# Re-ordering the second half of a fused RWKV6 + MLP kernel: a projection product in the front of a step, a multiplication inside the near products, and one chunk of unit 4 multiplied a step later

## The chip, the cores and the metric

The kernel runs on one core of one Trainium2 chip. The metric is the device time of one launch in microseconds. Three runs of the kernel before gave 609.04, 611.66 and 611.67 us, a median of 611.66 us. The execution that the profiler recorded took 610.0 us, with a span of 607.9 us from its first to its last instruction.

## The reference

Two blocks follow each other. The first is a linear attention with a decaying state, for 4 batches, 8 heads, 768 tokens and head size 48:

```python
for t in range(S):
    kt, vt, rt, wt = (k[:, :, t], v[:, :, t], r[:, :, t], w[:, :, t])
    cur = np.einsum('bhd,bhe->bhde', u[None] * kt, vt)
    y[:, :, t] = np.einsum('bhd,bhde->bhe', rt, state + cur)
    state = wt[:, :, :, None] * state + np.einsum('bhd,bhe->bhde', kt, vt)
```

Its output, seen as 3072 tokens by 384 features, is the input `x` of the second block, whose inner size is 2048:

```python
h = x @ w_in
sp = np.maximum(h, 0.0) + np.log1p(np.exp(-np.abs(h)))   # softplus
g = h * erf(sp)
return g @ w_out
```

Everything is float32.

## The kernel before, in words

**Units and steps.** The 3072 tokens are cut into 12 units of 256 tokens (two batches of 128 tokens each). One step of the main loop (line 1037) handles one unit of attention, and beside it the MLP of earlier units: in step s the attention of unit s runs, the hidden layer of unit s-1 (`hidden`, line 737) and the output projection of unit s-3 (`project_fast`, line 863, for units from 4 on; `project`, line 787, for the units before). Steps 0 to 4 use one schedule (`attend`), steps 5 to 11 another (`attend_late`, line 570). A tail after the loop finishes the last units. Only steps 5 to 11 are touched by the change.

**The order is written by hand.** The scheduler is off (line 1016), so each engine executes its instructions in the order in which the program issues them. `run_late` (line 967) reads strings of tokens from the tables `LATE` (line 950) and `USUAL` (line 962), one string for each of the places in a step at which `attend_late` calls `run`. The tokens are:

- P: one piece of the projection. In `project_fast` a unit has 7 pieces, each 8 products of 192 columns (line 878), which the trace shows as 16 matmul records. The pieces use two PSUM tiles `m`. Piece 1 is followed by a ScalarE copy (line 884), piece 3 by line 889, piece 4 by line 892, piece 6 by a VectorE addition (line 898) and piece 7 by another (line 902); the last two are followed by a store to HBM on SP's queue. In `project` a unit has 8 pieces, and pieces 6 and 8 are followed by a ScalarE copy (line 811).
- H: one piece of the hidden layer, 12 matmul records (line 770), then a ScalarE copy of 512 columns from PSUM tile `m` to `h` (line 779). A unit has 8. There are only two PSUM tiles `m`, so each H waits for the copy of the H before the last one, and the first two for the last readers of the projection's tiles.
- s, e, m: softplus (line 726), erf (line 730) and multiplication (line 735, VectorE) of one chunk of 1024 columns of `h`. A unit has 4 chunks; a chunk is complete after the 2nd, 4th, 6th and 8th H. Softplus and erf each come with a load of ScalarE's function table. The erf goes to a free PSUM room, called a lane: `ey` uses the tile `y`, `ep` uses the tile `pp1`. The next use of a lane waits for the multiplication that reads it. The first two chunks of a unit are worked on in the step of their H, the others in the step after.
- k: a ScalarE copy of a quarter of the activated unit to a lane (line 838). S: sums and differences of quarters on VectorE (lines 855 to 861), which `project_fast` needs because it forms the 2x2 block product with seven instead of eight products.
- F: the next part of the generator `prepare(s+1)` (line 267). T, G: one of four sums of quarters of `w_out`, on VectorE or GpSimd (line 826). A: one stage of the activation of a unit before 4.

**A step of `attend_late`, on TensorE.** It begins with what is called the front here: `from_own` with swap 1 for the unit before (line 484, 32 matmul records, into `y`), the level 5 products (line 450, 64 records), `from_own` with swap 0 (32 records), which may begin only when a small VectorE copy called the fence has read `y` (line 493), and `through_state` (line 510, 64 records). `from_own` with swap 1 overwrites `y`, so it waits for the last reader of that lane. The level 5 products wait for VectorE's scaling of level 4 (line 263), which is in the last part of `prepare`. Then come most of the P, the level 6 products (line 450) with `spread_blocks` (line 549), the last two P, the state products (line 536) and eight H.

**A step on VectorE.** After the fence it scales level 5 (line 263), takes the level (line 462), and then has a long row from `prepare(s+1)`, the near products: line 384, eight multiplications of distances 1 to 4 (lines 377 and 381), reductions of distances 1 to 3 (line 367), line 396 and two more reductions. GpSimd forms the products of distances 5 to 15 (the same two lines) and begins when the reductions of 1 to 3 have freed a room. Then come line 592 (`kT`), multiplications m, the scaling of level 6, the additions of the projection, the scalings of levels 1 to 3, S, further reductions and the scaling of level 4.

**A step on ScalarE.** It copies `y` to `xT` after `through_state` (lines 517 to 520), runs softplus and erf, copies `few` (line 555) and level 6 (line 469), copies quarters (line 838), and empties the tiles `m`.

**SP's queue** carries nearly all transfers. After `through_state` it issues six small transfers into `xT` (line 524) and then the loads of the next step (`load_step`).

Of the kernel before, what the change touches and what calls it, by code (L numbers as in the profile page):

```python
# [17 lines left out]
P = 128  # L18
# [21 lines left out]
DIRECT = 4  # L40
# [6 lines left out]
def view(ap, offset, dims):  # L47

    return bass.AP(ap.tensor, ap.offset + offset, [ap.ap[0], *dims])
# [12 lines left out]
def kernel(  # L62
# [107 lines left out]
    def near_log(s):  # L170
        return NEAR_LOG - (s == DIRECT)
# [76 lines left out]
    def rows(e, n=D):  # L248
        return slice(e * EP, e * EP + n)
# [17 lines left out]
    def prepare(s):  # L267
# [77 lines left out]
        front = att.tile([P, 2, JP, C], FP32, name="rk1", bufs=1)  # L345
        back = wide.tile([P, 2, DM, 2], I32, name="words", bufs=3)
        front = front[:].rearrange("p x n t -> p (x n t)")
        back = back[:].rearrange("p x n two -> p (x n two)").bitcast(FP32)
        terms, near = {}, 1 << near_log(s)
# [15 lines left out]
        def sum_up(*distances):  # L365
            for n in distances:
                nc.vector.tensor_reduce(  # L367
                    out=view(
                        sums[:], n, [[near * (NEAR + 1), NEAR // near], [NEAR + 1, near - n]]
                    ),  # L370
                    in_=terms[n], axis=mybir.AxisListType.X, op=ALU.add,
                )

        def term(engine, *distances):

            for n in distances:
                engine.tensor_mul(terms[n], r[:, :, n:], k[:, :, : near - n])  # L377

                m = near - n - (s == DIRECT)
                if m:  # L380
                    engine.tensor_mul(k[:, :, :m], k[:, :, :m], w[:, :, n : n + m])  # L381
# [3 lines left out]
        if near < NEAR:  # L385
            term(nc.vector, 1, 2, 3)
            yield
            term(nc.vector, 4, 5, 6, 7)
            nc.vector.tensor_mul(terms[0], terms[0], r)
            yield  # L390
            sum_up(*range(near))
        else:
            term(nc.vector, 1, 2, 3, 4)
            sum_up(1, 2, 3)
            term(nc.gpsimd, 5, 6, 7, 8)
            nc.vector.tensor_mul(terms[0], terms[0], r)
            sum_up(0, 4)
            term(nc.gpsimd, *range(9, NEAR))
# [145 lines left out]
    def spread_blocks(s, pp):  # L544
# [23 lines left out]
        )  # L568

    def attend_late(s, run):  # L570

        c, in_t, vt, own, S, S_next, ends = parts_of(s)
        RK = in_t[:, 0:2]
        before = s - 1 if s - 1 > DIRECT else None
        if before:
            from_own(before, ready[before][0], 1)
            fence()
        pp = products([P, NE, JP, HC], 0)
        level_products(pp, RK, LOG - 1)
        scale(s, LOG - 1)  # L580
        take_level(own, pp, LOG - 1)
        if before:
            from_own(before, ready[before][0], 0)
            through_state(before, xTs[before])
            if s + 1 < n_steps:
                load_step(s + 1)
        following = prepare(s + 1) if s + 1 < n_steps else iter(())
        next(following, None)
        nc.gpsimd.tensor_mul(faded[0][:], S[:], ends[:, :, 0:1].to_broadcast([P, JP, D]))
        next(following, None)  # L590
        kT = kTs[s]
        nc.vector.tensor_mul(
            kT[:].rearrange("p (e n) d -> p n e d", e=NE),
            kT[:].rearrange("p (e n) d -> p n e d", e=NE), spread[s][:],
        )
        run(0, following)

        pp = products([P, NE, JP, HC], 0)
        level_products(pp, RK, LOG)
        if s + 1 < n_steps:  # L600
            spread_blocks(s + 1, pp)
        take_level(own, pp, LOG)
        scale(s, LOG)
        run(1, following)
        ps = products([P, NC, JP, HC], 0)
        ps = [ps[:, h] for h in range(NC)]
        state_part(s, kT, ps)
        run(2, following)
        for e in range(NE):
            nc.vector.tensor_add(middle[rows(e)], faded[0][rows(e)], ps[0][rows(e), :, :D])  # L610
        run(3, following)
        if s < n_steps - SPC:
            nc.gpsimd.tensor_mul(
                faded[1][:], middle[:], ends[:, :, 1:2].to_broadcast([P, JP, D])
            )
            for e in range(NE):
                nc.vector.tensor_add(S_next[rows(e)], faded[1][rows(e)], ps[1][rows(e), :, :D])
        run(4, following)
# [318 lines left out]
    def in_order(s, k):  # L937
# [3 lines left out]
        for what in order[k]:  # L941
# [5 lines left out]
                piece(hids, s - 1)  # L947


    LATE = {  # L950
        DIRECT + 1: (
            "A P P P A P P", "F F F A P P P", "T", "H H F", "A s H ey m H H F G s H ep H H"
        ),
        DIRECT + 2: (
            "m s P P ey m P s P P ep m P", "k22y P F P k11p F F", "S1", "S2 S3 H k12y S4 H F",
            "s H ey m H H F G G s H ep H H",
        ),
        n_steps - 1: (
            "m s P ey m P s P P ep m P", "P P", "S", "H H", "s H ey m H H s H ep H H"
        ),  # L960
    }
    USUAL = (
        "m s P ey m P s P P ep m P", "k22y P F P k11p F F", "S1", "S2 S3 H k12y S4 H F",
        "s H ey m H H F s H ep H H",
    )

# [49 lines left out]
    with tc.manual_schedule(  # L1016
        engines={getattr(mybir.EngineType, x) for x in ("PE", "DVE", "Activation", "Pool", "SP")}
    ):
        warm = ps_m.tile([P, P], FP32, name="m")
        for _ in range(20):  # L1020
            nc.tensor.matmul(warm[:], lhsT=ident[:], rhs=ident[:], start=True, stop=True)  # L1021
        for t in (*states[0], *states[1], middle):
            nc.gpsimd.memset(t[:], 0.0)
        nc.gpsimd.memset(over_blocks[:], 1.0)
        nc.scalar.copy(u_row[:, :1], ident[:, :1])
        for _ in prepare(0):
            pass
        conversion = convert(
            [
                (into[:, f : f + 2, :], given[:, f : f + 2, :])  # L1030
                for into, given in ((w_in_sb, w_in), (w_out_sb, w_out))
                for f in range(0, NT, 2)
            ]
        )
        next(conversion)
        load_step(1)
        for s in range(n_steps):
            xTs[s] = xs.tile([P, KT, UNIT], FP32, name="xT")
            places = iter(range(8))

            def convert_at(n):
                if s < len(CONVERT) and n < len(CONVERT[s]):
                    for what in CONVERT[s][n]:
                        conversion.send(what)

            def place(n):
                if n == LOG - 1 and DIRECT - 1 <= s <= DIRECT:
                    load_rows(s + 2)
                for due in {(3, 4): (5,), (4, 3): (6,), (4, 5): (7,)}.get((s, n), ()):
                    load_w(due)  # L1050
                if s >= DIRECT:
                    in_order(s, next(places))
                    return
                if s in ALONE:
                    if s == 2 and not n:

                        next(hids[0])
                    convert_at(n)
                    advance(STAGES[s][n])
                elif s:  # L1060
                    advance(STAGES[s][n])
                    convert_at(n)
                else:
                    convert_at(n)
                beside(s, next(places))

            def run(n, following):
                if n == 3 and s < n_steps - 2:
                    load_rows(s + 2)
                if n == 3 and s + 3 < n_steps:  # L1070
                    load_w(s + 3)
                run_late(s, LATE.get(s, USUAL)[n], following)

            if s > DIRECT:
                attend_late(s, run)
                continue
            def behind(n=0):
                if n is not None:
                    convert_at(LOG + 2)
                    return  # L1080
                for what in BEHIND_SCALING:
                    conversion.send(what)

            attend(s, xTs[s], place, behind)
            if s + 2 < n_steps:
                load_step(s + 2)
                if s + 2 == DIRECT:
                    load_rows(s + 2)
        s = n_steps
        from_own(s - 1, ready[s - 1][0], 1)  # L1090
        fence()
        run_late(s, "s P")
        from_own(s - 1, ready[s - 1][0], 0)
        through_state(s - 1, xTs[s - 1])
        run_late(s, "m ey m P s P P ep m P P P S H H s H ey m H H s H ep m H H")
        run_late(s + 1, "s P ey m P s P P ep m P P P S")
        run_late(s + 2, "P P P P P P P")
# [96 lines left out]
```

## Time and profile before

| | |
|---|---|
| median of three runs | 611.66 us |
| the profiled execution, its own time | 610.0 us |
| its span | 607.9 us |
| TensorE matmul busy | 589.4 us, 97% of the span |
| VectorE, ScalarE, GpSimd busy | 442.9, 352.3, 281.4 us |
| start of the fronts of steps 6 to 11 | 249.97, 298.74, 345.25, 391.06, 436.85, 482.64 us |
| start of the tail | 526.57 us |

The profile names each instruction by its source line. "Busy" is the time in which an engine executes, and the idle time ahead of an instruction is put down to what released it. A releaser "issue" means that the engine waited for nothing that the profile shows. In the timelines the columns are the start in microseconds, the duration of the merged row, the engine, the line, the operation, what it writes and reads, the count, and in brackets the idle time ahead of the row with its releaser. The queue "q8 instruction" is not issued by the program[...].

### The profile page before, as it was taken

Reading aid. Unit: us, or ns where it says so; the run is one execution under the profiler, and the core shown is the slowest. Engines: PE = TensorE matmul, PEld = TensorE weight load, DVE = VectorE, ACT = ScalarE, POOL = GpSimd, SP = SyncE. Lnnn points to the kernel's source line nnn. Section 1 sums busy time; section 2 is a strip of 40 time slices with the busy share of each in tenths; the row PEclk is TensorE's granted clock in tenths of the full one; section 3 lists DMA queues with packets and bytes.
Section 4 is the critical chain, followed back from the end, with each engine's and each line's share of the span. In section 5 each row is a group of like instructions: output and inputs, shape, how many; then the busy total and the mean of one; then the engine's idle time right before and its main releaser. Section 6 shows DMA issues by size and latency. Waiting matters only on the chain.

```text
span 607.9 us, 16532 instructions
## 1 busy us (share of the span) xinstructions
PE 589.4 (97%) x7242; PEld 496.9 (82%) x7242; DVE 442.9 (73%) x508; ACT 352.3 (58%) x461; POOL 281.4 (46%) x298
## 2 busy tenths in 40 slices
PE   8889999999999999899999999999999999999997
PEld 7668787678668768658898799799898898898997
DVE  5688597895995898999899799799799634114140
ACT  2647887635536536456656666666756774655810
POOL 4348275602497489669749349349349100000000
PEclk9999999999999999899999999999999999999999
DMA  8376471441333413325324324333321300000000
GB/s 323 120 280 215 154 256 59 200 142 18 138 92 121 128 49 143 49 101 182 56 103 167 71 104 167 70 104 133 72 102 54 72 8 27 1 21 14 2 26 27
DMA packets 51376, 63.33 MB, mean 104 GB/s; under 512 B 34920, under 2 KB 40296, under 8 KB 49896
## 3 DMA queue, kind: packets, MB, share of 16 engines
q1 hardware_dynamic: 50824, 62.03, 31.6%
q8 instruction: 57, 0.93, 0.6%
q10 hardware_dynamic: 480, 0.25, 0.2%
q14 instruction: 15, 0.12, 0.1%
HBM read 52.39 MB, written 8.69 MB: 100 GB/s over the span
## 4 chain that ended last, share of the span: by engine, by line
PE 77%; DVE 14%; issue 5%; ACT 3%; POOL 1%; DMA 0%; DVEq 0%; ACTq 0%; POOLq 0%
PE m L770 35%; PE m L878 18%; PE m L802 11%; PE pp L450 6%; DVE in L263 3%; DVE words L381 2%; DVE sums L367 2%; PE y L484 2%; PE m L1021 1%; DVE rk L377 1%; PE y L510 1%; PE pp L536 1%; DVE own L462 1%; PE pp L675 1%; DVE h L735 1%
## 5 line engine op out<-in xcount | busy, mean ns | idle before, releaser
L770 PE MATMUL m<-xT,w_in_sb 128*128 128x256 f32 x1152 | 258.4, 382 | 4.6 <-DVE o L898 1.9
L770 PEld LDWEIGHTS m<-xT,w_in_sb 128*128 128x128 f32 x1152 | 215.6, 190 | 38.5 <-issue 3.5
L779 ACT COPY h<-m 128x512 f32<-128x512 f32 x96 | 55.6, 581 | 84.2 <-PE m L770 83.8
L263 DVE TENSOR_TENSOR in<-in,tot_sb 128x1024 f32<-128x1024 f32 (+1 forms) x60 | 84.7, 1411 | 18.7 <-PE pp L450 17.5
L381 POOL TENSOR_TENSOR words<-words,rest 128x528 f32<-128x528 f32 (+10 forms) x77 | 84.7, 1100 | 6.0
L802 PE MATMUL m<-w_out_sb,h 128*128 128x384 f32 x256 | 85.5, 490 | 0.0
L377 POOL TENSOR_TENSOR rk<-words 128x528 f32<-128x528 f32 (+3 forms) x28 | 35.4, 1264 | 92.3 <-DVE sums L367 81.9
L802 PEld LDWEIGHTS m<-w_out_sb,h 128*128 128x128 f32 x256 | 47.7, 190 | 31.7
L730 ACT ACT_TABLE_LOAD x32 | 41.1, 1283 | 25.7 <-DVE h L735 24.4
L450 PEld LDWEIGHTS pp<-in 48*64 48x64 f32 (+1 forms) x2368 | 34.8, 128 | 15.2 <-issue 8.3
L878 PE MATMUL m<-w_out_sb,h 128*128 128x192 f32 x256 | 44.9, 329 | 0.2 <-issue 0.2
L878 PE MATMUL m<-mixed,h 128*128 128x192 f32 x256 | 44.8, 328 | 0.0
L450 PE MATMUL pp<-in 48*64 48x64 f32 (+1 forms) x2368 | 39.5, 215 | 3.8 <-DVE in L263 1.5
L878 PEld LDWEIGHTS m<-w_out_sb,h 128*128 128x128 f32 x256 | 41.7, 190 | 1.0 <-issue 0.4
L735 DVE TENSOR_TENSOR h<-h,pp 128x1024 f32<-128x1024 f32 x16 | 19.5, 1216 | 31.1 <-ACT pp L730 31.1
L878 PEld LDWEIGHTS m<-mixed,h 128*128 128x128 f32 x256 | 41.7, 190 | 0.3
L726 ACT ACT_TABLE_LOAD x32 | 41.1, 1283 | 0.6
L315 POOL TENSOR_TENSOR tot_sb<-tot_sb 128x256 f32<-128x256 f32 (+4 forms) x60 | 38.1, 636 | 4.5
L377 POOL TENSOR_TENSOR words<-words 128x336 f32<-128x336 f32 (+6 forms) x49 | 38.2, 780 | 3.8
L735 DVE TENSOR_TENSOR h<-h,y 128x1024 f32<-128x1024 f32 x16 | 19.5, 1217 | 28.0 <-ACT y L730 27.8
L878 PE MATMUL m<-w_out_sb,room 128*128 128x192 f32 x224 | 38.7, 326 | 0.0
L878 PEld LDWEIGHTS m<-w_out_sb,room 128*128 128x128 f32 x224 | 36.8, 190 | 0.0
(123 smaller groups left out, 835.2 us busy)
## 6 DMA issues: line engine op xcount, KB each, us to landing
in<-in_rkw SPq DMA_DIRECT2D x11, 1024.0 KB, 5.1
words<-in_moe_w_in SPq DMA_DIRECT2D x8, 768.0 KB, 5.8
words<-in_moe_w_out SPq DMA_DIRECT2D x8, 768.0 KB, 4.6
words<-in_rk_rows SPq DMA_DIRECT2D x8, 768.0 KB, 5.6
w<-in_rkw SPq DMA_DIRECT2D x11, 512.0 KB, 7.0
v<-in_v SPq DMA_DIRECT2D x12, 384.0 KB, 6.2
out<-o SPq DMA_DIRECT2D x24, 192.0 KB, 2.6
rest<-in_w_rows SPq DMA_DIRECT2D x8, 384.0 KB, 6.0
```

The source lines that it names most:

```text
L263: nc.vector.tensor_mul(halves, halves, view(tots[level - 1], 0, [[1, n], [2, nb], [0, half]]))
L315: nc.gpsimd.tensor_mul(new, pair[:, :, 0], pair[:, :, 1])
L377: engine.tensor_mul(terms[n], r[:, :, n:], k[:, :, : near - n])
L381: engine.tensor_mul(k[:, :, :m], k[:, :, :m], w[:, :, n : n + m])
L450: nc.tensor.matmul(pp[s0 : s0 + m, e, n, :m], lhsT=rk[rows(e), 1, n, s0 : s0 + m], rhs=rk[rows(e), 0, n, t0 : t0 + m], start=True, stop=True,)
L726: nc.scalar.activation(sp_room, chunks[0], AF.Softplus)
L730: nc.scalar.activation(at, sp_room, AF.Erf)
L735: nc.vector.tensor_mul(h, h, at)
L770: nc.tensor.matmul(ps[:, ff, :], lhsT=w_in_sb[:, g * FG + f + ff, kk * P : (kk + 1) * P], rhs=xT[:, kk, :], start=kk == 0, stop=kk == KT - 1,)
L779: nc.scalar.copy(h[:, f : f + FT, :], ps[:])
L802: nc.tensor.matmul(ps[j][:], lhsT=gs[g][:, f, j * C : (j + 1) * C], rhs=w_out_sb[:, g * FG + f, :], start=g + f == 0, stop=g == NG - 1 and ...
L878: nc.tensor.matmul(to, lhsT=a[:, f], rhs=b[:, f], start=start and f == 0, stop=f == FG - 1, skip_group_check=True,)
```

## The change

The order of the work is changed in steps 5 to 11; no instruction of any engine is added or removed by its text.

- `prepare` gets one more stop, between the multiplications of distances 1 to 4 and the reductions, for steps from 6 on.
- `attend_late` calls `run` at two more places: "front", between the level 5 products and `from_own` with swap 0, and "near", at the new stop in `prepare`.
- In steps 6 to 11 the front now holds a softplus and one P. The multiplication of the second chunk of the unit, which was the first token after line 592, is now in "near". The last multiplication stands behind the level 6 scaling instead of ahead of it.
- In step 5 only one chunk of unit 4 is activated instead of two: its erf goes to lane `pp1` instead of `y`, and it is multiplied in step 6. The other three chunks of this unit each move one place on, so that the softplus and the erf of the last one stand among the last two P of step 6, and the lanes of step 6 are exchanged.

```diff
@@ -391,6 +391,8 @@
             sum_up(*range(near))
         else:
             term(nc.vector, 1, 2, 3, 4)
+            if s > DIRECT + 1:
+                yield
             sum_up(1, 2, 3)
             term(nc.gpsimd, 5, 6, 7, 8)
             nc.vector.tensor_mul(terms[0], terms[0], r)
@@ -579,6 +581,7 @@
         level_products(pp, RK, LOG - 1)
         scale(s, LOG - 1)
         take_level(own, pp, LOG - 1)
+        run("front", None)
         if before:
             from_own(before, ready[before][0], 0)
             through_state(before, xTs[before])
@@ -587,6 +590,8 @@
         following = prepare(s + 1) if s + 1 < n_steps else iter(())
         next(following, None)
         nc.gpsimd.tensor_mul(faded[0][:], S[:], ends[:, :, 0:1].to_broadcast([P, JP, D]))
+        next(following, None)
+        run("near", None)
         next(following, None)
         kT = kTs[s]
         nc.vector.tensor_mul(
@@ -947,20 +952,21 @@
+    STAGES_LATE = ("front", "near", 0, 1, 2, 3, 4)
     LATE = {
         DIRECT + 1: (
-            "A P P P A P P", "F F F A P P P", "T", "H H F", "A s H ey m H H F G s H ep H H"
+            "", "", "A P P P A P P", "F F F A P P P", "T", "H H F", "A s H H H F G ep H H H"
         ),
         DIRECT + 2: (
-            "m s P P ey m P s P P ep m P", "k22y P F P k11p F F", "S1", "S2 S3 H k12y S4 H F",
-            "s H ey m H H F G G s H ep H H",
+            "s P", "m", "ey P m s P P ep P m P", "s P P F ey m k22p k11y F F", "S1",
+            "S2 S3 H k12p S4 H F", "s H ey m H H F G G s H ep H H",
         ),
         n_steps - 1: (
-            "m s P ey m P s P P ep m P", "P P", "S", "H H", "s H ey m H H s H ep H H"
+            "s P", "m", "ey P m s P P ep P", "m P P", "S", "H H", "s H ey m H H s H ep H H"
         ),
     }
     USUAL = (
-        "m s P ey m P s P P ep m P", "k22y P F P k11p F F", "S1", "S2 S3 H k12y S4 H F",
+        "s P", "m", "ey P m s P P ep P", "m k22y P F P k11p F F", "S1", "S2 S3 H k12y S4 H F",
         "s H ey m H H F s H ep H H",
     )
@@ -1069,7 +1075,7 @@
-                run_late(s, LATE.get(s, USUAL)[n], following)
+                run_late(s, LATE.get(s, USUAL)[STAGES_LATE.index(n)], following)
```

`DIRECT` is 4, so the three entries of `LATE` are those of steps 5, 6 and 11, and `USUAL` is that of steps 7 to 10. The tail's strings are unchanged.

## The prediction

> **What bounds the kernel now.** I read the busy shares first, then TensorE's timeline of steps 9 and 10, then VectorE's and ScalarE's for the one wait that stands there, and last the boundary of steps 5 and 6. The page says that TensorE sets the time: it is busy in 97% of the span, at full clock nearly everywhere, so a gain can only come from its gaps.
>
> ```profile
> PE 589.4 (97%) x7242; PEld 496.9 (82%) x7242; DVE 442.9 (73%) x508; ACT 352.3 (58%) x461; POOL 281.4 (46%) x298
> PEclk9999999999999999899999999999999999999999
> q8 instruction: 57, 0.93, 0.6%
> ```
>
> TensorE's timeline from 384 to 478 us shows the step of about 45.8 us and three kinds of gap.
>
> ```profile
> 392.93 0.52 PE L510 MATMUL y<-in,s 48*48 48x64 f32 x24
> 394.67 0.32 PE L510 MATMUL y<-in,s 48*48 48x64 f32 x7 [1.23 <-issue]
> ...
> 459.28 0.92 PE L536 MATMUL pp<-v,kT 64*48 64x48 f32 x32
> 461.13 13.35 PE L770 MATMUL m<-xT,w_in_sb 128*128 128x256 f32 x60 [0.94 <-DVE o L898]
> 474.68 3.50 PE L770 MATMUL m<-xT,w_in_sb 128*128 128x256 f32 x15 [0.20 <-ACT h L779]
> ```
>
> (1) The front stops in the middle of equal small matmuls with the releaser "issue". Numbering TensorE's records in the trace (weight loads, matmuls, semaphores), the stops of steps 6 to 9 come after number 7617, 8641, 9665 and 10689, exactly 1024 apart. A q8 packet starts 2.3 to 2.4 us before each restart: 252.18, 301.00, 346.68, 392.30 us against restarts at 254.62, 303.33, 349.12, 394.67. There are 57 packets of 16 KB for 14,593 records, 256 each. So the next 256 instructions had not arrived. In the four stops the 256 records up to the restart took 3.1 to 3.6 us; the front's 192 weight-load and matmul pairs run at 15 ns each, 256 records in under 2 us, which is faster. Lost: 0.3, 0.3, 1.4 and 1.4 us.
>
> (2) The first H waits for VectorE's line 898. VectorE's and ScalarE's rows in step 10 say why it is late:
>
> ```profile
> 452.75 1.73 DVE L592 TENSOR_TENSOR kT<-kT,spread 128x768 f32<-128x768 f32 x1
> 454.40 1.21 DVE L735 TENSOR_TENSOR h<-h,pp 128x1024 f32<-128x1024 f32 x1
> 455.53 1.21 DVE L735 TENSOR_TENSOR h<-h,y 128x1024 f32<-128x1024 f32 x1
> 458.04 1.22 DVE L735 TENSOR_TENSOR h<-h,pp 128x1024 f32<-128x1024 f32 x1 [1.30 <-ACT pp L730]
> 459.17 1.44 DVE L263 TENSOR_TENSOR in<-in,tot_sb 128x512 f32<-128x512 f32 x1
> 460.54 0.54 DVE L898 TENSOR_TENSOR o<-o,m 128x384 f32<-128x384 f32 x1
> ```
>
> ```profile
> 455.68 1.28 ACT L730 ACT_TABLE_LOAD   x1 [4.93 <-DVE h L735]
> 456.98 1.03 ACT L730 ACTIVATE pp<-room 128x1024 f32<-128x1024 f32 x1
> ```
>
> The erf of the last chunk needs lane `pp1`, which the second chunk's multiplication frees only after all near products. ScalarE idles 4.93 us, then VectorE 1.30 us, and line 898 follows two instructions later. TensorE loses 1.1 us in steps 7 and 10. In steps 8 and 9 gap (1) has made TensorE late enough to hide this: the two gaps are rivals for the same time.
>
> (3) Into step 6, TensorE stands from 247.88 to 249.97 us, and again at 251.1:
>
> ```profile
> 249.97 0.90 PE L484 MATMUL y<-own,v 64*48 64x64 f32 x32 [1.94 <-DVE h L735]
> 251.13 1.99 PE L450 MATMUL pp<-in 48*64 48x64 f32 x64 [0.25 <-DVE in L263]
> ```
>
> ```profile
> 243.39 5.27 DVE L759 TENSOR_TENSOR h<-h,room 128x1024 f32<-128x1024 f32 x2
> 248.70 1.22 DVE L735 TENSOR_TENSOR h<-h,y 128x1024 f32<-128x1024 f32 x1
> 249.84 1.23 DVE L263 TENSOR_TENSOR in<-in,tot_sb 128x1024 f32<-128x1024 f32 x1
> ```
>
> `from_own` overwrites lane `y`, whose reader stands behind two slow multiplications; the level 4 scaling stands behind that reader. The windows show the price: a clock of 0.63 from 250 to 251 us and 0.50 from 251 to 253.
>
> [...] the trace has half clock for 3.41 us from 250.25 on, after only 2.1 us of idling. [...] line 759 took 3.29 us beside GpSimd's 3.44 us line 826, against its mean of 1.81.
>
> **The change part by part.** Nothing is added to any engine, so I lay the same rows out in the new order. T is the start of a front.
>
> *P in the front.* TensorE in a usual step: 0.48 + 0.93 (the first `from_own`, level 5), P 2.7, then 0.45 + 1.00, four P 10.6, level 6 and line 549 0.94, two P 5.4, state 0.87, H 20.92: together 44.3 us. A stretch of 256 instructions can no longer miss a P (2.7 us for 32 instructions): 2.7 + 224 x 7.5 ns = 4.4 us at least, above the 3.1 to 3.6 us that a block needs. All stops in fronts go: 0.3 + 1.4 + 1.4 = 3.1 us in steps 7 to 9. Splitting the row of P costs something: a P next to small tiles takes 2.80 us in the tail (row of line 878 at 527.16) against 2.64 in a row of five, so 0.2 us a step. What moves with it: the softplus stands in ScalarE's queue ahead of the `y` copies, but ScalarE idles there 2.3 to 3.8 us, and the copies wait for line 510 anyway. They come 2.7 us later, and so do SP's six transfers and `load_step` behind them: these end near T + 11, and H asks for `xT` at T + 23; the loads land about 5 us after issue and are asked for at T + 23 as well. No cost. GpSimd's queue isn't passed by these.
>
> *m inside the near products.* On VectorE line 592 begins at T + 15.9 now (452.75 - 436.85), then at T + 17.0. Behind it: 1.65 (kT), 1.13 (m), 1.38 (level 6 scaling), 1.13 (last m), 0.54 (line 898) = T + 22.9, against T + 24.2 now. The first H asks for its tile at T + 23.4. So gap (2) closes with 0.5 us to spare. The last erf: lane `pp1` is free at T + 12.2, line 892 waits for the fourth P until T + 13.9, table load and erf take 2.33, done at T + 16.3, and VectorE asks at T + 21.2. The copies k22 and k11 wait for the last m as before (T + 22.3; now 22.4). GpSimd's far products start 1.14 us later, and with them the reductions of their last terms; those lead to the level 4 scaling, which then has 2.3 us in hand. With VectorE 1.3 us earlier, the wait of 0.36 us inside H (steps 7 and 10) goes too.
>
> Steps 7 to 10 took 482.64 - 298.74 = 183.9 us. Now 4 x (44.3 + 0.2 + 0.1 for what small waits stay) = 178.4. **Minus 5.5 us.** Summed by gaps: 3.1 + 2.6 + 0.7 - 0.8 = 5.6.
>
> *Unit 4's first chunk a step later.* Step 5 no longer uses `y`, so `from_own` starts at 247.88. Level 5 still waits for line 263, which now follows line 759 directly: 248.70 to 249.93. TensorE idles 1.6 us there (from 248.36 to 249.98). This idling is between those of 1.4 us, after which the clock held, and the 2.1 us that halved it; I take full clock and keep 1.5 us for the other case. The front without P then takes 2.10 + 0.93 + 1.45 = 4.5 us, instead of 7.11 (247.88 to 254.99). With the split 0.2: **minus 2.4 us.**
>
> *The price in step 6.* The last chunk's erf now stands behind the copy of the eighth P (line 811) in ScalarE's queue. The P end at 274.4. Then line 811 to 275.0, table load and erf to 277.4, m to 278.6, k22 and k11 to 280.5, and only then the first H's line 779, to 281.1; the third H wants its tile at 280.5. The next copy, k12, waits for S1 (VectorE: scalings 3.1 to 3.5, S1 1.2, so 283), and the second H's copy stands behind it. Followed on, waits of 0.65, 0.7 to 1.0, 0.3 and 0.3: **plus 2.1 us**; bounds 0 (if ScalarE catches up) and 3.
>
> Step 11: no stop now, one split: plus 0.2. The tail: nothing. Sum: -5.5 - 2.4 + 2.1 + 0.2 = -5.6 us. On the profiled execution 610.0 - 5.6 = 604.4 us. The median of the runs is 1.66 above that execution and the mean of all four is 610.6; I say **605.0** for a median.
>
> **Rivals.**
> *More is gained (602.7):* step 6's queue costs nothing, -2.1. For it: in the old step 6 H ran without a gap. Against: the chain above has five links without slack.
> *Half is gained (608.0):* the spare 0.5 us before line 898 is used up, so a wait of about 0.9 us comes back at the first H in four steps (3.6 us less gain), or the half clock stays (1.5) and part of the fetch stops reappears elsewhere, the change then not doing what its front is shaped for. For it: in step 7 line 263 took 1.93 us instead of 1.23. Against: steps 8 to 10 agree to 0.1 us.
> *Slower (617):* GpSimd's far products, 1.14 us later, block two of VectorE's two-input instructions (lines 396, 592, 263) for 1.5 us each, as line 759 was blocked. Then line 898 is 3.0 us later in each of five steps, and 5 x (3.0 - 0.5) = 12.5 against 5.6 gained. It decides from 0.5 us a step, and the sign turns at 1.6. Against: these lines run beside the same GpSimd rows now, line 592 at 1.6 to 1.7 us.
>
> **How the numbers follow.** 605.0 (603.5 to 607): 0.55; 602.7: 0.18; 608.0: 0.20; slower: 0.07. The range 602.0 to 609.0 leaves out the slower case and the edges. About 0.5%, 3 us, can be told from no change; half of the third case falls inside. So faster 0.80, same 0.13, slower 0.07.
>
> **What would show it.** Right: no "issue" gap in the fronts of lines 484 to 510, steps 7 to 10 at 44.6 us, line 898 ended before line 536 ends, 1.6 us ahead of level 5 in step 6, waits for line 779 in step 6's H. Wrong: an "issue" gap at another line, a first H that waits for line 898, or half clock after step 5.

## The result, and the profile after

| | before | changed |
|---|---|---|
| median of six runs | 610.14 us (609.04 to 611.67) | 605.58 us (603.82 to 607.62) |
| profiled execution, its own time | 610.0 us | 603.8 us |
| its span | 607.9 us | 602.0 us |
| mean TensorE clock in it (1.0 is full clock) | 0.997 | 1.0 |

The ratio is 0.9922, with a 95% interval of 0.9894 to 0.995: 0.8% faster. In the changed kernel the lines from 394 on have moved by 2, those from 582 on by 3, those from 590 on by 5 and those of the tables and behind them by 6: the level 5 and 6 products are now line 452, `from_own` 486, `through_state` 512, softplus 731, erf 735, the multiplication m 740, the two multiplications of a token A 764, the H matmuls 775 and their copy 784, the products of `project` 807 and its copy 816, the copy of a quarter 843, the first sum of quarters 860, the products of `project_fast` 883, its copy behind piece 3 894 and its first addition 903.

The page after, with TensorE's share one point higher:

```profile
PE 588.4 (98%) x7242; PEld 495.4 (82%) x7242; DVE 440.4 (73%) x508; ACT 353.5 (59%) x461; POOL 289.4 (48%) x298
PEclk9999999999999999999999999999999999999999
```

TensorE's timeline of step 10 after (start, duration, line, count, idle ahead in brackets):

```profile
431.88 0.66 PE L486 MATMUL y<-own,v 64*48 64x64 f32 x32
432.37 1.11 PE L452 MATMUL pp<-in 48*64 48x64 f32 x64
433.41 2.87 PE L883 MATMUL m<-w_out_sb,h 128*128 128x192 f32 x16
436.21 0.66 PE L486 MATMUL y<-own,v 64*48 64x64 f32 x32
...
454.63 0.92 PE L538 MATMUL pp<-v,kT 64*48 64x48 f32 x32
455.48 19.69 PE L775 MATMUL m<-xT,w_in_sb 128*128 128x256 f32 x90
```

No bracket is left in the step, and in steps 7 to 11 no idle time of TensorE is longer than 0.15 us: the front has a P in its middle and no stop, H follows the state products at once. VectorE's row of the same step shows why:

```profile
442.99 1.21 DVE L740 TENSOR_TENSOR h<-h,pp 128x1024 f32<-128x1024 f32 x1
...
448.92 1.72 DVE L597 TENSOR_TENSOR kT<-kT,spread 128x768 f32<-128x768 f32 x1
450.56 1.21 DVE L740 TENSOR_TENSOR h<-h,y 128x1024 f32<-128x1024 f32 x1
451.69 0.68 DVE L263 TENSOR_TENSOR in<-in,tot_sb 128x512 f32<-128x512 f32 x1
452.30 1.21 DVE L740 TENSOR_TENSOR h<-h,pp 128x1024 f32<-128x1024 f32 x1
453.43 0.54 DVE L903 TENSOR_TENSOR o<-o,m 128x384 f32<-128x384 f32 x1
```

The row has no idle time any more, and line 903 ends at 453.97 us, 1.5 us before H asks for its tile. The boundary into step 6, and step 6's H, on TensorE:

```profile
247.71 0.66 PE L486 MATMUL y<-own,v 64*48 64x64 f32 x32
250.01 1.16 PE L452 MATMUL pp<-in 48*64 48x64 f32 x64 [1.64 <-DVE in L263]
...
281.50 2.86 PE L775 MATMUL m<-xT,w_in_sb 128*128 128x256 f32 x12 [0.43 <-ACT h L784]
284.55 13.73 PE L775 MATMUL m<-xT,w_in_sb 128*128 128x256 f32 x60 [0.20 <-ACT h L784]
```

`from_own` starts as soon as H ends; level 5 waits 1.64 us for the scaling. The third and the fourth H wait visibly for ScalarE's copies (each H is 12 matmuls). From start to start, the H up to the sixth lose 0.59, 0.46, 0.25 and 0.26 us from the third on.

### The profile page after: what moved, and what is told of

It reads as the page before. It is cut to its first block, busy times and chain, and to the rows that moved or that the text cites. A ratio compares the mean times of both kernels' runs of the same rounds, so it can differ in the third digit from the quotient of the medians.

```text
span 602.0 us, 16529 instructions
## 1 busy us (share of the span) xinstructions
PE 588.4 (98%) x7242; PEld 495.4 (82%) x7242; DVE 440.4 (73%) x508; ACT 353.5 (59%) x461; POOL 289.4 (48%) x298
## 4 chain that ended last, share of the span: by engine, by line
PE 70%; DVE 10%; POOL 10%; issue 4%; DMA 4%; ACT 2%; SPq 0%; POOLq 0%; DVEq 0%; ACTq 0%
PE m L775 32%; PE m L883 25%; PE m L807 4%; PE pp L452 4%; POOL words L381 3%; DMA w<-in_rkw 3%; POOL tot_sb L315 2%; DVE in L263 2%; PE y L486 2%; POOL rk L377 2%; POOL words L377 1%; DVE words L381 1%; PE y L512 1%; DVE h L764 1%; PE pp L538 1%
## 5 line engine op out<-in xcount | busy, mean ns | idle before, releaser
L263 DVE TENSOR_TENSOR in<-in,tot_sb 128x1024 f32<-128x1024 f32 (+1 forms) x60 | 80.1, 1335 | 23.6 <-PE pp L452 20.8
L381 POOL TENSOR_TENSOR words<-words,rest 128x528 f32<-128x528 f32 (+10 forms) x77 | 80.8, 1050 | 6.0
L377 POOL TENSOR_TENSOR rk<-words 128x528 f32<-128x528 f32 (+3 forms) x28 | 41.5, 1481 | 81.8 <-DVE sums L367 71.4
L315 POOL TENSOR_TENSOR tot_sb<-tot_sb 128x256 f32<-128x256 f32 (+4 forms) x60 | 43.8, 730 | 4.6
L377 POOL TENSOR_TENSOR words<-words 128x336 f32<-128x336 f32 (+6 forms) x49 | 36.6, 746 | 3.8
L367 DVE TENSOR_REDUCE sums<-rk 128x14 f32<-128x672 f32 (+9 forms) x54 | 34.7, 702 | 0.0
```

What stands on the lines that cost most here:

```text
L263: nc.vector.tensor_mul(halves, halves, view(tots[level - 1], 0, [[1, n], [2, nb], [0, half]]))
L315: nc.gpsimd.tensor_mul(new, pair[:, :, 0], pair[:, :, 1])
L367: nc.vector.tensor_reduce(out=view(sums[:], n, [[near * (NEAR + 1), NEAR // near], [NEAR + 1, near - n]]), in_=terms[n], axis=mybir.AxisLi ...
```

## The experiments

My theory after the result was that of the prediction: two gaps, late instructions in the front and VectorE's row ahead of the projection's addition, hide each other, and the gain needs both closed; unit 4's part is a near balance of a gain and a loss. The rivals were that one part alone makes the whole gain. A bracket counts idle time from the modelled end of the matmul before it, so a loss counted from start to start, as I give it below where I say that TensorE loses time, is about 0.2 us longer. In the lists of periods, a period runs from the end of one step's H to the end of the next one's.

**E1: all but the P in the front.** In the strings of steps 6 to 11:

```diff
-        "s P", "m", "ey P m s P P ep P", "m k22y P F P k11p F F",
+        "s", "m", "P ey P m s P P ep P", "m k22y P F P k11p F F",
```

> The changed kernel with one thing undone: the P goes back behind line 512 (through_state) in steps 6 to 11; the softplus stays in the front and the multiplication inside the near products. My theory (two gaps that hide each other, instruction arrival in the front and VectorE's row before the projection's addition, both closed by the change): stops without a releaser come back in the fronts, at records of TensorE that leave 193 when divided by 256, 1.3 to 1.5 us in two of the steps 7 to 10 and less in others; no first H waits for the addition; four steps 7 to 10 together 180 to 181 us instead of 178.2; span about 604. Rival 'the front P is the whole gain': steps 7 to 10 back at 183 to 184 us, span about 607. Rival 'the moved multiplication is the whole gain': 178 us, span about 602.

Ratio to the kernel before 0.9941 (0.9918 to 0.9964), span 604.9 us, periods of steps 7 to 10: 44.19, 45.55, 45.70, 44.20, together 179.6, a little under the 180 to 181 expected. TensorE in step 9:

```profile
391.58 0.52 PE L512 MATMUL y<-in,s 48*48 48x64 f32 x24
393.40 0.32 PE L512 MATMUL y<-in,s 48*48 48x64 f32 x7 [1.30 <-issue]
```

The stop is back, at the same place in the program as before. TensorE loses 1.36 us in step 8 and 1.51 us in step 9, 0.99 us in step 6, each behind record 193 of a block of 256 of its instructions; each restart comes 2.3 to 2.6 us after the start of a packet of the instruction queue (391.01 us for the stop shown). The two steps without a stop take 44.2 us, 0.3 us less than in the changed kernel: that is what the split of the P costs. If the P in the front were the whole gain, the four periods would be those of before, near 45.9 us; if it brought nothing, those of the changed kernel, near 44.5. Here the steps that stop are as long as before and the others are not: without the P the gain depends on where the blocks of instructions happen to begin and end.

**E2: only the P in the front.** The kernel before, with its first P moved:

```diff
-        "m s P ey m P s P P ep m P", ...
+        "P", "", "m s ey m P s P P ep m P", ...
```

> The kernel before with one part of the change alone: the first P of steps 6 to 11 stands in the front, everything else (multiplications, softplus, step 5, lanes) in the old order. My theory: no stop without a releaser in any front of steps 6 to 11, but now the first H waits for VectorE's addition by about 0.9 us in each of the steps 7 to 10, and H waits again by 0.3 to 0.5 us; these four steps take 45.5 to 45.8 us each, 182 to 183 us together (183.9 before), span 606.5 to 607.5. Rival 'the front P is the whole gain': steps 7 to 10 at 44.6 us each, span 604 to 604.5.

Ratio 1.0014 (0.9996 to 1.0031): no gain. Span 608.2 us, periods 46.05, 45.82, 45.79, 45.81, together 183.5 where I expected 182 to 183. No front stops, as expected, but I had the place of the new wait wrong. TensorE in step 7, and ScalarE beside it:

```profile
309.21 2.76 PE L883 MATMUL m<-mixed,room 128*128 128x192 f32 x16
312.74 2.87 PE L883 MATMUL m<-w_out_sb,room 128*128 128x192 f32 x16 [0.77 <-ACT o L894]
```

```profile
305.26 1.28 ACT L731 ACT_TABLE_LOAD   x1
...
311.27 1.06 ACT L731 ACTIVATE room<-h 128x1024 f32<-128x1024 f32 x1
312.23 0.46 ACT L894 COPY o<-m 128x384 f32<-128x384 f32 x1
```

With one P fewer behind the `y` copies, TensorE reaches the fifth P before ScalarE has done softplus, erf and softplus (seven microseconds in a row) and the copy of line 894 behind them. TensorE loses 0.93 us there in every step, and this delay hides most of the wait for VectorE's addition. The softplus in the front, which I had counted as free, takes 2.35 us out of exactly this row. E8, which has it there, no longer shows this wait. That the changed kernel would wait here without it is likely, but no run has both other parts without the softplus.

**E8: softplus and P in the front, the multiplications of steps 7 to 10 put back.**

```diff
-        "s P", "m", "ey P m s P P ep P", "m k22y P F P k11p F F",
+        "s P", "", "m ey P m s P P ep m P", "k22y P F P k11p F F",
```

> The changed kernel with the multiplications of the steps 7 to 10 put back: the second chunk's behind line 597 (kT) and the last one ahead of the level 6 scaling; the softplus and the P stay in the front. My theory: no stop in the fronts and no wait inside the P (the softplus is out of ScalarE's way), but VectorE's row before the projection's addition is long again: ScalarE idles over 4 us until lane pp1 is free, VectorE 1.3 us for the erf, and the first H waits 0.8 to 0.9 us for the addition, then 0.3 to 0.5 us inside H; steps 7 to 10 take 45.6 to 45.8 us each, span 606 to 607. Rival (with the softplus in the front the chain has time enough): the steps stay at 44.5 us, span 602.

One execution. Periods 46.23, 45.77, 45.77, 45.79, within the expectation but for the first. Step 9 on VectorE and on TensorE:

```profile
413.03 1.22 DVE L740 TENSOR_TENSOR h<-h,pp 128x1024 f32<-128x1024 f32 x1 [1.30 <-ACT pp L735]
414.16 1.43 DVE L263 TENSOR_TENSOR in<-in,tot_sb 128x512 f32<-128x512 f32 x1
415.51 0.54 DVE L903 TENSOR_TENSOR o<-o,m 128x384 f32<-128x384 f32 x1
```

```profile
414.60 0.94 PE L538 MATMUL pp<-v,kT 64*48 64x48 f32 x64
416.11 2.21 PE L775 MATMUL m<-xT,w_in_sb 128*128 128x256 f32 x9 [0.57 <-DVE o L903]
```

This is gap (2) of the prediction, now in all four steps: brackets of 0.57 to 0.92 us ahead of the first H, and eight H that take 21.52 us instead of 20.92. It costs as much as the stops did. The span of 609.0 us is above the 606 to 607 that I expected, mostly because this execution was 1.6 us later already at the H of step 5, where the program is that of the changed kernel.

**E4: TensorE's instructions shifted by 128.** The kernel before, with 64 matmuls more in step 5 that write the same values again:

```diff
         level_products(pp, RK, LOG)
+        if s == DIRECT + 1:
+            level_products(pp, RK, LOG)
```

> The kernel before with the level 6 products of step 5 issued twice (64 more matmul records with their weight loads, 128 more instructions of TensorE, the same values written again). My theory (the stops are late instructions, in blocks of 256 counted from the start of the program): they still come at records that leave 193 when divided by 256, so they leave the fronts of steps 7, 8 and 9 and appear in the fronts of steps 10 and 11, 1 to 1.5 us each; in steps 8 and 9 the first H waits about 1 us for VectorE's addition instead, so these steps stay at 45.6 to 45.8 us; span 608.5 to 610. Rival (the stops belong to their place in the program: a wait on data or a semaphore in line 510): they stay in steps 8 and 9 at line 510, with 1.4 us each.

One execution, span 607.2 us, below the 608.5 to 610 expected. The lines behind the edit have moved by 2: H is line 772 here, the projection's products 880, its first addition 900. The fronts of steps 7, 8 and 9 have no stop any more; these steps show instead what the stops had covered (step 8), and a stop stands behind the front of step 10:

```profile
366.94 0.94 PE L536 MATMUL pp<-v,kT 64*48 64x48 f32 x64
368.80 3.50 PE L772 MATMUL m<-xT,w_in_sb 128*128 128x256 f32 x15 [0.93 <-DVE o L900]
...
439.00 0.43 PE L880 MATMUL m<-w_out_sb,h 128*128 128x192 f32 x1
440.04 2.22 PE L880 MATMUL m<-w_out_sb,h 128*128 128x192 f32 x12 [0.61 <-issue]
```

The stop is behind record 11969 = 46 x 256 + 193, in another line (880) than before (510). So it belongs to the count of instructions and not to a place in the program. It lost 0.88 us from start to start, less than the 1 to 1.5 expected, as its block ended just behind the front. In step 11, where I expected another, the block took 3.4 us and ended inside the P: no stop. The periods of steps 7 to 10 are 45.78, 45.79, 45.80 and 45.78, with or without a stop.

**E3: unit 4 as before.** Step 5 with two chunks and lane `y`, step 6 in the usual pattern:

```diff
-            "", "", "A P P P A P P", ..., "A s H H H F G ep H H H"
+            "", "", "A P P P A P P", ..., "A s H ey m H H F G s H ep H H"
-            "s P", "m", "ey P m s P P ep P m P", "s P P F ey m k22p k11y F F", "S1",
-            "S2 S3 H k12p S4 H F", ...
+            "s P", "m", "ey P P m s P P ep P", "m k22y P F P k11p F F", "S1",
+            "S2 S3 H k12y S4 H F", ...
```

> The changed kernel with unit 4 activated as before: step 5 works on two chunks again and uses lane y, step 6 follows the usual pattern of the new order. My theory: the front of step 6 starts 2.1 us late again behind the multiplication that reads y, level 5 waits again; the front (without its P, counted from the end of the last H) takes 5.5 us at full clock or about 7 with half clock instead of 4.9; in return step 6's H run without waits, 20.9 instead of 22.6 us. Net against the changed kernel: -0.8 us at full clock to +0.8 with half clock, span 601.2 to 602.8. Rival 'unit 4's later chunk brought a good part of the gain': span 604 or more.

Ratio 0.9907 (0.9877 to 0.9936). The one run at a mean clock of 1.0 took 603.98 us; the two such runs of the changed kernel took 603.82 and 603.97. So at full clock, as far as one such run tells, this part of the change is worth nothing: what the front wins, step 6's H give back (they take 20.92 us here). The profiled execution is no help on this: its span of 604.1 us (mean clock 0.994) lies above my 601.2 to 602.8 and where the rival put it, but it had half clock for 6.8 us from 250.2 us on, twice as long as the kernel before, and its other steps agree with the changed kernel (steps 7 to 10: 44.53, 44.53, 44.53 and 44.51 us). The medians of all runs, 605.64 and 605.58 us, show no difference either.

**E5: the last erf of step 6 ahead of the eighth P.**

```diff
-"s P P F ey m k22p k11y F F"
+"s P ey P F m k22p k11y F F"
```

> The changed kernel with one token moved in step 6: the last chunk's erf stands ahead of the eighth P and so ahead of the copy that waits for this P. My theory (the 1.7 us that step 6's H wait are ScalarE's queue behind that copy): the eight H of step 6 take 20.9 to 21.2 us instead of 22.6, span 600.3 to 600.7. Rival (they wait for VectorE's sums, whatever ScalarE does): the H stay at 22 us or more, span about 602.

Step 6's H take 20.92 us from the first start to the start of the next front, instead of 22.60, and no wait is left in them; span 600.5 us:

```profile
275.56 20.99 PE L775 MATMUL m<-xT,w_in_sb 128*128 128x256 f32 x96
```

So ScalarE's queue behind line 816 was the whole cause of the waits in step 6. Ratio to before 0.9922 (0.9897 to 0.9946); the five runs scatter from 602.48 to 607.36 us with mean clocks from 1.0 down to 0.991.

**E6: the last A in the front of step 6.** In step 5 `"A s H H H F G ep H H H"` becomes `"s H H H F G ep H H H"`, in step 6 `"s P"` becomes `"A s P"`.

> The changed kernel with the last token A moved from step 5 to the front of step 6: the two multiplications of 1024 columns that stood ahead of the level 4 scaling come after the taking of level 5, when GpSimd is idle. My theory: level 5 of step 6 no longer waits (1.6 us less), the two multiplications take 1.3 us each instead of 2.0 and 3.3, the near products start about 1 us later after the last H, which VectorE's wait of 3.6 us later in the step takes up; span 600.3 to 600.6. And if this idling is what sometimes brings the half clock, the runs' mean clock stays at 1.0 and their times stay within 1 us (603.8 to 607.6 for the changed kernel). Rival: the scattering of the runs has another source and stays.

Ratio 0.9887 (0.9871 to 0.9904), span 600.6 us, four runs within 602.65 to 602.75 us at mean clocks of 0.999 and 1.0. TensorE and VectorE at the boundary:

```profile
247.49 0.67 PE L486 MATMUL y<-own,v 64*48 64x64 f32 x32
247.98 1.11 PE L452 MATMUL pp<-in 48*64 48x64 f32 x64
249.02 2.85 PE L807 MATMUL m<-w_out_sb,h 128*128 128x384 f32 x8
```

```profile
242.93 3.30 DVE L263 TENSOR_TENSOR in<-in,tot_sb 128x1024 f32<-128x1024 f32 x1
...
250.92 2.36 DVE L764 TENSOR_TENSOR h<-h,room 128x1024 f32<-128x1024 f32 x2
```

Level 5 no longer waits, and the two multiplications take 2.36 us together instead of 5.27. The reason that I had given for this is wrong: GpSimd is not idle there.

```profile
250.94 1.26 POOL L315 TENSOR_TENSOR tot_sb<-tot_sb 128x16 f32<-128x16 f32 x1
252.16 1.22 POOL L338 TENSOR_TENSOR over_blocks<-tot_sb 128x16 f32<-128x16 f32 x1
```

The multiplications start at 250.92 and 252.05 us, just ahead of these two, and it is GpSimd's short instructions that take longer (line 338 took 0.24 us in the kernel before). In step 5 the first multiplication had started behind a GpSimd instruction of 3.43 us instead. The four runs no longer scatter, now that the idle time is gone.

**E7: E5 and E6 together.**

> Both moves together, the version that should beat both kernels: level 5 of step 6 without a wait and the H of step 6 at 20.9 to 21.4 us; span 598.8 to 599.5, and if TensorE no longer idles over 1 us after step 5, all runs at a mean clock of 1.0, 600.5 to 601.5 us; at least 1.5% below the kernel before.

Ratio 0.9888 (0.9872 to 0.9904), median of five runs 602.68 us, span 600.7 us: 1.1% below the kernel before, but no better than E6 alone, and the 598.8 to 599.5 us that I expected fell. The front is as in E6, but the H of steps 6 and 7 take 21.93 and 21.91 us. VectorE in step 6:

```profile
275.77 3.81 DVE L263 TENSOR_TENSOR in<-in,tot_sb 128x1024 f32<-128x1024 f32 x2
279.50 1.21 DVE L860 TENSOR_TENSOR room<-h,pp 128x1024 f32<-128x1024 f32 x1
...
294.15 3.31 DVE L426 TENSOR_TENSOR own<-block_sb,by_tokens 128x1024 f32<-128x1024 f32 x1 [1.08 <-DMA by_tokens<-by_blocks]
```

E5 has the same order in ScalarE's queue and H without waits. There the first of these rows took 3.24 us, and line 860 began 4.2 us after the first H of the step; in E7 it began 5.4 us after it (279.50 less 274.06). ScalarE's copy of a quarter waits for line 860, and the copy of the second H stands behind it. TensorE gets there 1.5 us earlier than in E5, VectorE only 0.3 us. That VectorE has become the bound there is read from these rows; no run takes them apart, so this cause stays open.

## Why the prediction was right, step by step

The median was predicted at 605.0 us and came at 605.58 us. The signs named for being right were all seen. Of those for being wrong the profile shows none; half clock is likely in most of the other runs (see below).

- **Steps 7 to 10:** minus 5.5 us predicted (178.4 us), 178.2 us measured (298.22 to 476.40). Both mechanisms are shown: E1 and E4 for the late instructions, E8 for VectorE's row, E2 for ScalarE's row, which takes their place when the P alone is moved.
- **No stop with a P in the front:** the blocks that contain a front took 4.51 to 4.63 us in steps 6 to 11, against at least 4.4 us estimated. But the 3.1 to 3.6 us that I took for what a block needs is no fixed need: in steps 10 and 11 before, a whole block passed in 1.82 and 1.80 us without a stop (see the last section). The P was long enough where it counted, in steps 6 to 9.
- **VectorE's row:** line 903 ends at T + 22.1 where I had T + 22.9; the H ask at T + 23.6 (predicted 23.4). The term that was too large is the level 6 scaling, 0.68 us instead of 1.38 (see below). The spare time is 1.5 us, not 0.5, so the rival that used it up had less room than I gave it.
- **The split:** 0.3 us a step (E1 against the changed kernel), not 0.2. Step 11 grew by 0.33 us.
- **Softplus in the front:** I called it free. It is, and E2 and E8 show that it also removes a wait of 0.77 us, which I had not seen.
- **The front of step 6:** 4.9 us without its P (247.71 to 255.37 less 2.78), 4.7 predicted, 7.11 before. More than half of this gain is chance: the profile before had half clock here, and E2's profile, with the same step 5, had not; its front took 5.8 us without the P. At full clock this part then wins 0.9 us at the front, less than the 1.7 us that step 6's H lose.
- **Step 6's H:** plus 2.1 us predicted, 1.68 measured (22.60 less 20.92), by the named queue: E5 removes all of it. The term that was too large is mainly the wait of the fourth H, 0.46 us against 0.7 to 1.0.
- **Sum:** -5.7 - 2.2 + 1.7 + 0.3 = -5.9 us, the difference of the spans (602.0 and 607.9); -5.6 predicted. That it agrees so closely is in part luck, as the one span has half clock and the other has not. The medians differ by 4.6 us.
- **Full clock after step 5:** this assumption held in the profiled execution and not in general. The mean clocks of the six runs are 1.0, 0.994, 0.996, 1.0, 0.991 and 0.997, with times of 603.8, 607.0, 605.5, 604.0, 607.6 and 605.7 us in the same order. The case for which I kept 1.5 us is thus the usual one, and it fits that the median lies 1.8 us above the profiled execution. In E6 and E7, without the idle time, eight of nine runs had 0.999 or 1.0. That the half clock lies behind step 5 in the unprofiled runs is inferred from this, not seen.
- **The slower rival**, my estimate from line 759 alone (3.29 us against a mean of 1.81), needed 1.6 us more in VectorE's row per step; the row became shorter.

## What to carry to other kernels

When an engine is busy 97% of the time, count its gaps by the place at which they come back, and ask of each what it hides: here two gaps of about 1.4 us shared the same time, the P alone brought nothing, the change without the P 0.6% (two of its steps happened not to stop), and both together 0.8%. The front, a stretch of many very short matmuls, outran its own instructions here, with stops of up to 1.5 us; one longer piece of other work in its middle cured that, at 0.3 us a step. A part that is balanced at best (unit 4 here) should be looked at for what it moved into a queue: moving one erf and one token A afterwards took 1.5 and 1.4 us off the span, though not both at once.

## What the runs showed of the hardware

- **Late instructions.** In the ten traces TensorE stops 31 times for 0.15 us or more with the releaser "issue", at the start of the kernel too. All 31 come behind record 193 of a block of 256 TensorE instructions, and each ends 2.2 to 2.6 us after the start of a 16 KB packet of the instruction queue. So in these traces the end of a stop goes with the start of that packet. In step 8 before, the block ahead of the stop began at 345.92 us, inside the front, and the packet 0.8 us later (346.68). In step 10 a block began with the front itself, at 436.86 us, and the packet had started 2.9 us before that (433.96): its 256 instructions went by in 1.82 us without a stop.

```profile
437.34 1.11 PE L450 MATMUL pp<-in 48*64 48x64 f32 x64
438.27 0.63 PE L484 MATMUL y<-own,v 64*48 64x64 f32 x32
438.72 0.63 PE L510 MATMUL y<-in,s 48*48 48x64 f32 x32
```

- **Beside GpSimd the same scaling took 0.68 or 1.44 us, by the order of the starts.** The level 6 scaling (128 x 512) took 1.44 us in step 10 before, when it started at 459.17 us behind a GpSimd multiplication of 459.06, and 0.68 us after, when it started at 451.69, ahead of GpSimd's of 451.78. Here is GpSimd before, then after:

```profile
459.06 1.00 POOL L381 TENSOR_TENSOR words<-words,rest 128x384 f32<-128x384 f32 x1
...
451.78 1.55 POOL L377 TENSOR_TENSOR rk<-words 128x432 f32<-128x432 f32 x1
```

  The second then took 1.55 us, against 1.10 for the same shape before. The other steps repeat it: 1.44 or 1.45 us in each of steps 6 to 10 before, where the scaling started 0.10 to 0.11 us behind the GpSimd multiplication and ended 0.55 us behind its end; 0.68 us in each of them after, started 0.09 to 0.13 us ahead of the next GpSimd instruction. A row's duration next to GpSimd is therefore not a constant that can be carried to another order.
- **In these traces the half clock went with where the idle time fell.** Ahead of the front of step 6 and of its level 5, the profile before idled 1.94 and 0.25 us and E3 1.94 and 0.26 us; they then had half clock for 3.41 and 6.83 us. E2, whose step 5 is that of the kernel before, idled 1.95 and 0.49 us and kept full clock:

```profile
250.41 0.66 PE L486 MATMUL y<-own,v 64*48 64x64 f32 x32 [1.95 <-DVE h L740]
251.56 1.16 PE L452 MATMUL pp<-in 48*64 48x64 f32 x64 [0.49 <-DVE in L263]
```

  In all ten traces the changes of clock lie whole multiples of 3.413 us apart (before: 242.35 us of full clock, which is 71 of them, then 3.41 of half clock). Counted on from E2's first clock record, at 7.20 us, a point of this grid falls at 249.55 us and cuts the idle time of 1.95 us into 1.1 and 0.9. In before and in E3 the clock changed at 250.25 and 250.21 us, just after the longer idle time, which thus lay whole in one stretch. E4 idled only 1.39 and 0.48 us, both inside one stretch (248.16 to 251.57), and had half clock for 3.41 us behind it. So in these four traces the length of the idle time alone does not decide, and the grid lies differently in each execution. That fits the scatter of the runs' mean clocks. Why most other runs of the changed kernel, which idles only 1.64 us there in its profile, show a lower mean clock is not seen.
